# First stage of a long convolution with two MLPs: each step's load in three transfers

## Chip, cores and metric

One Trainium2 chip, one NeuronCore. The metric is the device time of one execution in microseconds (us).

## What is computed

The reference, cut to what matters:

```python
def _attn_ref(x, v, pos_emb, w1, w2):            # x, v: (2, 12480, 128); pos_emb: (12480, 64)
    h_filt = (np.maximum(pos_emb @ w1, 0.0) @ w2) * np.exp(-0.01 * pos)[:, None]
    u = x * v
    y = irfft(rfft(u, n=2 * S, axis=1) * rfft(h_filt, n=2 * S, axis=0), n=2 * S, axis=1)[:, :S]
    return x * y

h = attn_out.reshape(24960, 128) @ w_in;  out1 = np.square(np.maximum(h, 0)) @ w_out
h = out1 @ w_in2;                         out  = (h * np.cos(h)) @ w_out2
```

All arrays are float32. The sequence of 12,480 positions is transformed as 104 by 120 (`N1` by `N2`).

## The kernel before, in words

**Three stages.** The first stage makes the convolution's inputs (u = x*v and the filter h_filt, from a small MLP over the positions) and takes the transform over 104 rows. The second stage takes the transform over 120 rows, multiplies the spectra and transforms back. The third runs the last transform and the two MLPs in one long loop. Between the stages the data goes through tensors in device memory, `Bs` and `Ds`.

**The first stage** has 30 steps q (`NCH`) of two pairs each (`CB`), so 60 pairs. `load` (lines 163 to 169) brings a step's data from device memory: a tile of 128 rows, a row being 2,672 float32 = 10,688 bytes. Columns 0 to 2463 (`XVE`) hold x, v and the transform's matrix of the step and have meaning in rows 0 to 103 only; rows 104 to 127 are padding there. The last 208 columns hold the positions' features, in all 128 rows. The tiles are a ring of five slots (`LDB`): the load of step q+5 is issued right behind the second pair of step q and waits until that pair has read the slot.

The work of a step is spread over the loop (lines 260 to 285):
- `mlp1` (line 182, TensorE, then ScalarE's Relu on line 184) reads the positions. For step q it runs about three pairs behind the issue of the step's load.
- `prep` reads x and v (line 192, GpSimd's product u) and makes h_filt (line 194, TensorE; line 196, ScalarE). Its first product for step q stands four pairs ahead of that step's first pair.
- `pair` multiplies with the transform's matrix (line 210, TensorE, into three tiles `A` of PSUM), copies one half (line 212, ScalarE) and forms sum and difference (line 214, VectorE).
- `store` (line 219) writes a step's result to `Bs` as two transfers, 128 and 80 rows of 6,144 bytes. They are issued from ScalarE's own queue, between its other instructions.
- Between the pairs VectorE, ScalarE and GpSimd split the MLPs' weights; 16 transfers `wr` (line 87) of 512 KB load them.

**Order.** Each engine executes its instructions in the order of the program, and a DMA issue stands in that order too: what waits ahead of a store on ScalarE, or ahead of a load on SP, holds up all that stands behind it. Every transfer from SP and ScalarE counts on one of eight semaphores (DMAHW0 to DMAHW7), given out in turn. A transfer waits until the one that had its semaphore before has landed.

Of the kernel before, what the change touches and what calls it, by code (L numbers as in the profile page):

```python
# [21 lines left out]
N1, N2, HB = 104, 120, 60  # L22
# [3 lines left out]
NCH, CB = 30, 2  # L26
# [15 lines left out]
KE = 32  # L42
FIRST = 384 + 4 * NCH + 2 * KR
XVE, SLOT = 2048 + 2 * KR, 3072
CROSS = (1, 1)
WS = 59
INV2PI = 0.15915494309189535
# [10 lines left out]
def conv_moe(ctx, tc, t):  # L58
    nc = tc.nc
# [70 lines left out]
    def slot(name, pool=ring, size=SLOT):  # L130
        return pool.tile([128, size], F32, tag="ld", name=name)
# [16 lines left out]
    with ExitStack() as st:  # L148
# [12 lines left out]
        ld = {}  # L161

        def load(q):
            sl = slot("ld", *((ring, SLOT) if q % LDB < NB else (ring1, XVE + CB * N1)))
            nc.sync.dma_start(out=sl[:, 0:XVE + CB * N1], in_=t["ld"][q])
            x, v = (sl[0:N1, 1024 * n:1024 * (n + 1)].rearrange("p (i a d) -> p i a d", i=CB, a=2) for n in range(2))
            et = sl[0:N1, 2048:XVE].rearrange("p (a m) -> p a m", a=2)
            pt = sl[:, XVE:XVE + CB * N1].rearrange("p (i k) -> p i k", i=CB)
            ld[q] = (pt, x, v, et)
# [76 lines left out]
        def last():  # L246
            direct(NCH - 1, 1, 0)
            direct(NCH - 1, 1, 1, nc.scalar)
            store_late(NCH - 1)

        upto("load", load, LDB, NCH)
        nc.sync.dma_start(out=Bs[0:KE, CB * LATE:HB].rearrange("p x e -> p (x e)"),
                          in_=bass.AP(t["ld"].tensor, 0, [[CB * (NCH - LATE) * 768, KE], [1, CB * (NCH - LATE) * 768]]))
        nc.scalar.dma_start(out=Gt, in_=t["G"])
        nc.scalar.dma_start(out=It, in_=t["IG"])
        for n, (q, i) in enumerate(seq):
            lead = min(LA, n + 1) if n else 1
            upto("mlp", mlp1, (n + lead - 1) // CB + 1, NCH)
            upto("prep", lambda m: prep(*seq[m]), n + lead, len(seq))
            pair(q, i, last if n == len(seq) - 1 else None)  # L260
            upto("mlp", mlp1, (n + lead + 1) // CB + 1 if n else 1, NCH)
            if i == 0 and q:
                if q > LATE:
                    store_late(q - 1)
                if q < NCH - 1:
                    store(q - 1)
            if (q, i) == (LATE, 0):
                load2(0)
                load2(1)
            if (q, i) == (NCH - 1, 0):  # L270
                load_late(0, CB * (NCH - 1 - LATE))
                direct(q, 0, 0)
                direct(q, 0, 1)
            if (q, i) == (NCH - 1, 1):
                load_late(1)
                load2(2)
                store(q - 1, nc.sync)
                store(q, nc.sync)
                load_late(2)
            if i == 1:  # L280
                upto("load", load, q + LDB + 1, NCH)
            if 1 < n < WS:
                decode(2)
# [22 lines left out]
    with ExitStack() as st:  # L306
# [33 lines left out]
        def crossed(g, j, c):  # L340
            return (j, c) == CROSS and g < NG - 1

# [375 lines left out]
def tables():  # L718
    import numpy as np
    s1, k1, s2 = np.arange(N1), np.arange(N1), np.arange(N2)  # L720
    b, kk = np.arange(HB), np.arange(HB)
    n = N2 * s1[:, None, None] + s2[None, :, None]
    th = 2 * np.pi * (((4 * k1[None, None, :] - 1) * n) % (4 * S)) / (4 * S)
    E = np.stack([np.cos(th), -np.sin(th)], 2)
    T = E.transpose(3, 1, 2, 0) / S
    E = E.reshape(N1, 2, HB, 2, N1).transpose(2, 0, 1, 4, 3).reshape(HB, N1, 2 * KR)
    G = np.zeros((2 * HB, 2, 128))
    I = np.zeros((128, 2, 2 * HB))
    for c in range(2):
        p = 2 * np.pi * ((2 * b[:, None] * kk[None, :] + b[:, None] * c) % N2) / N2  # L730
        C, Z = np.cos(p), np.sin(p)
        for n, o in enumerate(turns()):
            re, im = (HB + n, n) if n % CB and n > 1 else (n, HB + n)
            G[re, c, 0:60], G[im, c, 0:60] = C[o], Z[o]
            G[re, c, 64:124], G[im, c, 64:124] = -Z[o], C[o]
        I[0:60, c, 0::2], I[64:124, c, 0::2] = C.T, -Z.T
        I[0:60, c, 1::2], I[64:124, c, 1::2] = Z.T, C.T
    f = lambda a: np.ascontiguousarray(a, dtype=np.float32)
    win = np.exp(-0.01 * np.arange(S, dtype=np.float32))
    first = np.zeros((128, FIRST))  # L740
    first[0:N1, 384 + 4 * NCH:] = E[NCH]
    win = paired(win.reshape(N1, 2, HB), 0, 2).transpose(0, 2, 3, 1)
    first[0:N1, 384:384 + 4 * NCH] = win.reshape(N1, 4 * NCH)
    return {"E": f(E[0:NCH]), "first": f(first), "G": f(G), "IG": f(I)}, T
# [6 lines left out]
def paired(a, rows, pairs):  # L751
    import numpy as np
    a = np.take(a, turns(), pairs)
    a = a.reshape(a.shape[:pairs] + (NCH, CB) + a.shape[pairs + 1:])
    m = np.moveaxis(a, (pairs, pairs + 1, rows), (0, 1, 2)).copy()
    m[1:, 1] = m[1:, 1, ::-1]
    return np.moveaxis(m, (0, 1, 2), (pairs, pairs + 1, rows))


def host(inp):  # L760
    import numpy as np
    c = np.ascontiguousarray
    out, T = tables()
    out["T"] = c(T.astype(np.float32).reshape(N1, N2 // CI, CI, 2, N1).transpose(1, 0, 2, 3, 4))
    a = inp["x"].reshape(2, N1, N2 // CI, CI, D)
    out["xT"] = c(a.transpose(2, 4, 3, 0, 1)).reshape(N2 // CI, D, CI, UT)
    for s, d in (("x", "xl"), ("v", "vl")):
        a = paired(inp[s].reshape(2, N1, 2, HB, D), 1, 3)
        out[d] = c(a.transpose(3, 1, 4, 2, 0, 5)).reshape(NCH, N1, 1024)
    xve = np.concatenate([out.pop("xl"), out.pop("vl"), out.pop("E")], 2)  # L770
    p = paired(inp["pos_emb"].reshape(N1, 2, HB, 64), 0, 2)
    pos = c(p.transpose(2, 1, 4, 3, 0)).reshape(NCH, 128, CB * N1)
    out["ld"] = np.concatenate([np.pad(xve, [(0, 0), (0, 128 - N1), (0, 0)]), pos], 2)
    for a in range(2):
        out["first"][64 * a:64 * a + 64, 64 * a:64 * a + 64] = inp["w1"]
        out["first"][64 * a:64 * a + 64, 128 + 128 * a:256 + 128 * a] = inp["w2"]
    for n in _W:
        out[n] = c(inp[n]).view(np.int64)
    return out
# [22 lines left out]
```

## Time and profile before

| | us |
|---|---|
| median of 3 runs (lowest, highest) | 2743.23 (2742.17, 2744.23) |
| profiled execution, first to last instruction (its span) | 2739.5 |
| TensorE busy in the span | 2693.9 (98%) |
| VectorE busy | 2387.9 (87%) |
| ScalarE busy | 2383.4 (87%) |
| GpSimd busy | 1351.7 (49%) |

For the profiled execution the span is all that is recorded of its time; the median of the runs is 3.7 us above it. Busy shares are means over stages with different limits: the first stage is about the first 223 us, the second ends at about 480 us, the rest is the MLPs. A profile has 16 DMA engines; a DMA share of 1 says that all 16 have work all the time.

### The profile page before, as it was taken

The numbers are of one execution on the slowest core, as the hardware profiler recorded it, in microseconds if no ns is written. First come the engines' busy times: TensorE is split into PE (matmuls) and PEld (weight loads), VectorE is DVE, ScalarE is ACT, GpSimd is POOL, SyncE is SP. The second block draws the span as 40 slices with busy tenths as digits, with TensorE's granted clock in tenths as the row PEclk, the third lists the DMA queues.
The fourth block names the chain that finished last, engine by engine and source line by source line (L and its number), as shares of the span: only waits on it lengthen the run. The fifth ranks groups of instructions, "written<-read, shape, count | busy, mean of one in ns | idle before, by whom it ended". The sixth has DMA issues, their size and how long they took to land.

```text
span 2739.5 us, 38808 instructions
## 1 busy us (share of the span) xinstructions
PE 2693.9 (98%) x11778; PEld 2112.1 (77%) x11778; DVE 2387.9 (87%) x4675; ACT 2383.4 (87%) x4295; POOL 1351.7 (49%) x1050
## 2 busy tenths in 40 slices
PE   8898999999999999999999999999999999999999
PEld 5554444888888888888888888888888888888887
DVE  5886999788888888888888888888888888888888
ACT  4445998799999999999999999999999999999998
POOL 4554888144444444444444444444444444444445
PEclk9999999999999999999999999999999999999999
DMA  9997997210101110101010101010001110101000
GB/s 380 393 396 260 297 297 243 84 31 16 35 26 32 29 33 16 35 26 32 28 32 17 38 23 32 29 32 29 31 18 32 29 32 29 32 17 32 17 8 10
DMA packets 86771, 219.64 MB, mean 80 GB/s; under 512 B 6025, under 2 KB 49633, under 8 KB 82689
## 3 DMA queue, kind: packets, MB, share of 16 engines
q1 hardware_dynamic: 79298, 180.24, 20.2%
q10 hardware_dynamic: 7263, 36.92, 3.4%
q8 instruction: 93, 1.52, 0.2%
q14 instruction: 117, 0.96, 0.1%
HBM read 140.37 MB, written 77.07 MB: 79 GB/s over the span
## 4 chain that ended last, share of the span: by engine, by line
PE 92%; DMA 5%; ACT 1%; DVE 1%; issue 1%; POOL 0%; SPq 0%; POOLq 0%; ACTq 0%; DVEq 0%
PE h L562 13%; PE h L564 13%; PE y L578 13%; PE h L563 13%; PE y L576 13%; PE y L577 13%; PE pc L528 4%; DMA ld<-ld 3%; PE d L385 3%; PE Z L345 3%; PE A L210 3%; PE H L317 2%; PE hp L194 1%; DMA B<-Bs 1%; PE hp L182 0%
## 5 line engine op out<-in xcount | busy, mean ns | idle before, releaser
L667 POOL TENSOR_TENSOR gl<-g,gh 128x512 fp32r<-128x512 f32 (+2 forms) x800 | 1040.6, 1301 | 1221.5 <-ACT gh L658 718.1
L650 DVE TENSOR_TENSOR g<-h,c 128x512 f32<-128x512 f32 (+2 forms) x800 | 537.7, 672 | 209.4 <-ACT c L642 196.9
L627 ACT ACTIVATE k<-h,quarter 128x512 int32<-128x512 f32 (+2 forms) x800 | 540.3, 675 | 122.0 <-PE h L564 118.8
L562 PE MATMUL h<-zh,wh 128*128 128x512 f32 (+2 forms) x1600 | 625.5, 391 | 1.2 <-DVE zh L546 0.9
L578 PE MATMUL y<-gl,wh 128*128 128x512 f32 (+2 forms) x1600 | 617.6, 386 | 4.3 <-POOL gl L667 2.5
L576 PE MATMUL y<-gh,wl 128*128 128x512 f32 (+2 forms) x1600 | 616.4, 385 | 0.1
L564 PE MATMUL h<-zh,wl 128*128 128x512 f32 (+2 forms) x1600 | 615.6, 385 | 0.0
L563 PE MATMUL h<-zl,wh 128*128 128x512 f32 (+2 forms) x1600 | 614.7, 384 | 0.0
L577 PE MATMUL y<-gh,wh 128*128 128x512 f32 (+2 forms) x1600 | 614.1, 384 | 0.0
L642 ACT ACTIVATE c<-r,halfpi 128x512 f32<-128x512 f32 (+2 forms) x800 | 565.3, 707 | 2.6 <-DVE r L635 2.6
L621 DVE TENSOR_TENSOR gl<-g,gh 128x512 fp32r<-128x512 f32 (+2 forms) x800 | 534.6, 668 | 1.1
L635 DVE CUSTOM_DVE_ANT_0 r<-h,k 128x512 f32<-128x512 f32 (+2 forms) x800 | 534.1, 668 | 0.0
L601 ACT ACTIVATE r<-h 128x512 f32<-128x512 f32 (+2 forms) x800 | 471.9, 590 | 69.4 <-PE h L564 57.8
L607 ACT ACTIVATE g<-r 128x512 f32<-128x512 f32 (+2 forms) x800 | 492.8, 616 | 1.0 <-DVE gl L621 0.4
L614 DVE CAST gh<-g 128x512 fp32r<-128x512 f32 (+2 forms) x800 | 330.4, 413 | 38.5 <-ACT g L607 35.6
L578 PEld LDWEIGHTS y<-gl,wh 128*128 128x128 f32 x1600 | 300.4, 188 | 70.4 <-POOL gl L667 7.7
L576 PEld LDWEIGHTS y<-gh,wl 128*128 128x128 f32 x1600 | 300.5, 188 | 60.7 <-DVE zl L589 1.2
L564 PEld LDWEIGHTS h<-zh,wl 128*128 128x128 f32 x1600 | 300.9, 188 | 59.9
L577 PEld LDWEIGHTS y<-gh,wh 128*128 128x128 f32 x1600 | 300.7, 188 | 59.4
L562 PEld LDWEIGHTS h<-zh,wh 128*128 128x128 f32 x1600 | 301.5, 188 | 56.8 <-issue 1.0
L563 PEld LDWEIGHTS h<-zl,wh 128*128 128x128 f32 x1600 | 301.2, 188 | 54.8
L658 ACT ACTIVATE gh<-g 128x512 fp32r<-128x512 f32 (+2 forms) x400 | 246.1, 615 | 0.1
(67 smaller groups left out, 2424.9 us busy)
## 6 DMA issues: line engine op xcount, KB each, us to landing
ld<-ld SPq DMA_DIRECT2D x30, 1336.0 KB
B<-Bs SPq DMA_DIRECT2D x25, 1536.0 KB
dt<-Ds SPq DMA_DIRECT2D x59, 416.0 KB
Ds<-dt SPq DMA_DIRECT2D x24, 960.0 KB
Bs<-bt ACTq DMA_DIRECT2D x28, 768.0 KB
Bs<-bt ACTq DMA_DIRECT2D x28, 480.0 KB
xt<-xT SPq DMA_DIRECT2D x60, 208.0 KB
out<-o SPq DMA_DIRECT2D x47, 256.0 KB
```

Source lines behind the costliest of these rows:

```text
L562: nc.tensor.matmul(h[:, :n], wh[:, f, :], zh[:, :n], start=True, stop=False)
L563: nc.tensor.matmul(h[:, :n], wh[:, f, :], zl[:, :n], start=False, stop=False)
L564: nc.tensor.matmul(h[:, :n], wl[:, f, :], zh[:, :n], start=False, stop=True)
L576: nc.tensor.matmul(y[:, :n], wl[:, f, :], gh[:, :n], start=a, stop=False)
L577: nc.tensor.matmul(y[:, :n], wh[:, f, :], gh[:, :n], start=False, stop=False)
L578: nc.tensor.matmul(y[:, :n], wh[:, f, :], gl[:, :n], start=False, stop=b)
L621: nc.vector.tensor_tensor(out=gl[:, :n], in0=g[:, :n], in1=gh[:, :n].bitcast(F32), op=ALU.subtract)
L627: nc.scalar.activation(k[:, :n], hp[2, u][:, :n], AF.Identity, scale=-1.0, bias=quarter)
L635: nc.vector._custom_dve(TENSOR_ADD_SAT, out=r[:, :n], in0=h[:, :n], in1=k[:, :n], s0=0.25, s1=-0.75)
L642: nc.scalar.activation(c[:, :n], r[:, :n], AF.Sin, bias=halfpi, scale=TWO_PI)
L650: nc.vector.tensor_tensor(out=g[:, :n], in0=h[:, :n], in1=c[:, :n], op=ALU.mult)
L667: nc.gpsimd.tensor_tensor(out=gl[:, :n], in0=g[:, :n], in1=gh[:, :n].bitcast(F32), op=ALU.subtract)
```

## The change

`load` issues three transfers in place of one: the positions (128 rows of 832 bytes, from a tensor `pos` of their own), then rows 0 to 95 of the other columns (`EVEN` is 96; rows of 9,856 bytes), then rows 96 to 103. The 24 rows of padding are gone from the host's tensor and from the transfer. Nothing else differs.

```diff
--- before.py
+++ after.py
@@ -42,6 +42,7 @@
 KE = 32
 FIRST = 384 + 4 * NCH + 2 * KR
 XVE, SLOT = 2048 + 2 * KR, 3072
+EVEN = N1 - N1 % 16
 CROSS = (1, 1)
 WS = 59
 INV2PI = 0.15915494309189535
@@ -162,7 +163,9 @@
 
         def load(q):
             sl = slot("ld", *((ring, SLOT) if q % LDB < NB else (ring1, XVE + CB * N1)))
-            nc.sync.dma_start(out=sl[:, 0:XVE + CB * N1], in_=t["ld"][q])
+            nc.sync.dma_start(out=sl[:, XVE:XVE + CB * N1], in_=t["pos"][q])
+            nc.sync.dma_start(out=sl[0:EVEN, 0:XVE], in_=t["ld"][q, 0:EVEN])
+            nc.sync.dma_start(out=sl[EVEN:N1, 0:XVE], in_=t["ld"][q, EVEN:N1])
             x, v = (sl[0:N1, 1024 * n:1024 * (n + 1)].rearrange("p (i a d) -> p i a d", i=CB, a=2) for n in range(2))
             et = sl[0:N1, 2048:XVE].rearrange("p (a m) -> p a m", a=2)
             pt = sl[:, XVE:XVE + CB * N1].rearrange("p (i k) -> p i k", i=CB)
@@ -770,7 +773,7 @@
     xve = np.concatenate([out.pop("xl"), out.pop("vl"), out.pop("E")], 2)
     p = paired(inp["pos_emb"].reshape(N1, 2, HB, 64), 0, 2)
     pos = c(p.transpose(2, 1, 4, 3, 0)).reshape(NCH, 128, CB * N1)
-    out["ld"] = np.concatenate([np.pad(xve, [(0, 0), (0, 128 - N1), (0, 0)]), pos], 2)
+    out["ld"], out["pos"] = xve, pos
     for a in range(2):
         out["first"][64 * a:64 * a + 64, 64 * a:64 * a + 64] = inp["w1"]
         out["first"][64 * a:64 * a + 64, 128 + 128 * a:256 + 128 * a] = inp["w2"]
```

On SP's queue the first stage looks as follows. `ld` is a step's tile, `wr` a weight tile; the brackets name the semaphores that a row waits for, and a DMAHW there is the one that the transfer then counts on itself, or that of the data it needs. Before, from the load of step 9 on:

```order
L165 DMA ld<-ld 128x2672 [waits DMAHW0_49,DMAHW7_49,PE_49,Pool_49]
L87 DMA wr<-moe_w_in 128x1024 [waits DMAHW1_49,DVE_49]
L165 DMA ld<-ld 128x2672 [waits DMAHW3_49,DMAHW4_49,PE_49,Pool_49]
L87 DMA wr<-moe_w_out 128x4x256 [waits DMAHW6_49,DMAHW2_49,DVE_49]
L165 DMA ld<-ld 128x2672 [waits DMAHW0_49,PE_49,Pool_49]
L165 DMA ld<-ld 128x2672 [waits DMAHW3_49,PE_49,Pool_49]
```

With the change, the same place:

```order
L166 DMA ld<-pos 128x208 [waits DMAHW2_49,PE_49,Pool_49]
L167 DMA ld<-ld 96x2464 [waits DMAHW3_49]
L168 DMA ld<-ld 8x2464 [waits DMAHW5_49]
L88 DMA wr<-moe_w_in 128x1024 [waits DMAHW7_49,DVE_49]
L166 DMA ld<-pos 128x208 [waits DMAHW0_49,PE_49,Pool_49]
L167 DMA ld<-ld 96x2464 [waits DMAHW2_49]
L168 DMA ld<-ld 8x2464 [waits DMAHW4_49]
L88 DMA wr<-moe_w_out 128x4x256 [waits DMAHW5_49,DVE_49]
```

Each load has become three issues. The first carries the wait for the slot (PE, Pool); each has a semaphore of its own and waits for that semaphore's last holder.

On ScalarE's queue, at a store between two pairs; `hT` is the Relu of `mlp1`, `Bs` the store, `ut` and `v` are the copies for the next pairs. Before:

```order
L184 ACTIVATE hT<-hp 128x208 [waits PE_49]
L219 DMA Bs<-bt 128x1536 [waits DMAHW5_49,DVE_49]
L219 DMA Bs<-bt 80x1536 [waits DMAHW7_49]
L196 ACTIVATE ut<-hp_466,first 104x128 [waits PE_49]
L196 ACTIVATE ut<-hp_466,first 104x128
L212 ACTIVATE v<-A 128x768 [waits PE_49,Activation_49]
L196 ACTIVATE ut<-hp_487,first 104x128 [waits PE_49,Pool_49]
```

With the change:

```order
L187 ACTIVATE hT<-hp 128x208 [waits PE_49]
L222 DMA Bs<-bt 128x1536 [waits DMAHW1_49,DVE_49]
L222 DMA Bs<-bt 80x1536 [waits DMAHW3_49]
L199 ACTIVATE ut<-hp_488,first 104x128 [waits PE_49]
L199 ACTIVATE ut<-hp_488,first 104x128
L215 ACTIVATE v<-A 128x768 [waits PE_49,Activation_49]
L199 ACTIVATE ut<-hp_511,first 104x128 [waits PE_49,Pool_49]
```

The order is the same. The semaphores are others: with five to six transfers a step in place of three to four, a semaphore's last holder is about one and a half steps back, where it was more than two. The store of 80 rows, which waits for DMAHW3 here, follows on that semaphore the load of rows 0 to 95 that stands second in SP's rows above. Over the first stage, 13 of the 28 stores of 80 rows follow a load of rows 0 to 95 in this way and 4 one of rows 96 to 103; of the 30 loads of rows 0 to 95, 15 follow a store of 80 rows. Before, no store of 80 rows followed a load; 18 of the 28 stores of 128 rows did, one that was issued more than two steps earlier.

## Rows read from the trace of the kernel before

**Rows 1.** the page: 40 slices of the span, and the chain's shares

```profile
DMA  9997997210101110101010101010001110101000
...
PE 92%; DMA 5%; ACT 1%; DVE 1%; issue 1%; POOL 0%; SPq 0%; POOLq 0%; ACTq 0%; DVEq 0%
```

**Rows 2.** busy time by stretch of the span; the columns are its first line

```profile
core 0: us, PE busy (x) PEld busy (x) DVE busy (x) ACT busy (x) POOL busy (x), PEclk, DMA share, GB/s
0.00:223.00 223.00, 196.31 (x635) 119.15 (x636) 173.25 (x220) 101.59 (x224) 115.69 (x94) 0.98 0.98 382
```

**Rows 3.** DMA queues, 40 to 205 us: packets, MB, share of 16 engines' time

```profile
q1 hardware_dynamic: 7729, 36.93, 59.0%
q10 hardware_dynamic: 5273, 28.09, 41.5%
...
ld<-ld SPq DMA_DIRECT2D x22, 1336.0 KB
```

**Rows 4.** chain that ended last, 36 to 64 us: start, length, what

```profile
40.71 2.60 PE A L210 x8
...
43.36 10.72 DMA ld<-ld
...
54.13 0.62 PE hp L182 x2
...
55.18 2.58 PE A L210 x8
...
58.20 2.58 PE A L210 x8
...
61.56 2.60 PE A L210 x8
```

**Rows 5.** PE's groups, 0 to 223 us: busy, mean ns, idle before, releasers

```profile
L182 PE MATMUL hp<-ld,first 128*128 128x208 f32 x60 | 17.9, 382 | 24.5 <-DMA ld<-ld 16.6 <-DMA first<-first 7.9
```

**Rows 6.** DMA queues, 7 to 22 us: the first loads

```profile
q1 hardware_dynamic: 648, 6.03, 97.1%
```

**Rows 7.** DMA queues, 9 to 17 us: short rows (Gt, It) on q10

```profile
q10 hardware_dynamic: 213, 0.18, 6.7%
```

**Rows 8.** DMA, 602 to 605.2 us: one transfer of 104 rows of 1,664 bytes

```profile
DMA packets 117, 0.17 MB, mean 54 GB/s; under 512 B 13, under 2 KB 117, under 8 KB 117
...
q1 hardware_dynamic: 117, 0.17, 19.1%
```

**Rows 9.** DMA, 605.3 to 610 us: a transfer of 128 rows, one of 104

```profile
DMA packets 574, 0.65 MB, mean 138 GB/s; under 512 B 29, under 2 KB 573, under 8 KB 573
...
dt<-Ds SPq DMA_DIRECT2D x1, 416.0 KB
xt<-xT SPq DMA_DIRECT2D x1, 208.0 KB
```

**Rows 10.** DMA, 717 to 718.8 us: mainly 128 rows of 1,664 bytes

```profile
q1 hardware_dynamic: 131, 0.21, 38.8%
```

**Rows 11.** the SP queue's waits, 40 to 205 us: total, times, longest

```profile
SPq L165 <- PE A L210: 122.6, 22, 10.4
```

**Rows 12.** line 165: its issues, ns min/median/max

```profile
L165 SPq DMA_DIRECT2D ld<-ld x30: 327/328/647, 0.7 to 201.0; - x30
```

**Rows 13.** waits of the engines, 40 to 205 us: total, times, longest

```profile
ACT hT L184 <- PE hp L182: 35.9, 22, 3.9
POOL ut L192 <- PE A L210: 15.7, 8, 3.3
```

## Prediction

> **What bounds the kernel now.** I read first the page: which stretch keeps the DMA engines busy, and what the chain that ended last consists of. TensorE makes up 92% of that chain and DMA 5%; the DMA engines are full in the first slices only [rows 1]. So the change, which touches the first stage alone, can move the time only by what it does there, and a later end of that stage is passed on: behind it TensorE fills the chain.
>
> Next, the first stage by itself. In its 223 us the DMA engines are busy 0.98 of the time and move 382 GB/s, while TensorE is busy 196.3 us, VectorE 173.3, GpSimd 115.7 and ScalarE 101.6 [rows 2]. From 40 to 205 us SP's queue (loads and weights) takes 59.0% of the engines' time and ScalarE's (stores) 41.5%, together all of it; 22 loads are issued there, one in 165 / 22 = 7.5 us [rows 3]. Third, the chain inside that stage: a pair ends, the load for its slot goes out, 10.72 us later it has landed, `mlp1` runs at once, and pairs follow 3.02 and 3.36 us apart until the next load [rows 4]. TensorE lost 16.6 us to such landings [rows 5]. The stage is therefore bound by the transfers' volume; TensorE alone would do a step of two pairs in 6.38 us [rows 4].
>
> **What the change removes.** Per load and engine, in steps:
> - Before: 128 rows on 16 engines are 8 rows of 10,688 bytes each. While loads ran nearly alone, 6.03 MB took 97.1% of 16 engines for 15 us, 233 us of engine time, so an engine moves 25.9 KB per us [rows 6]. A row takes 0.413 us, the 8 take 3.30 us.
> - Positions now: 8 rows of 832 bytes for each engine. The nearest row is that of the short rows of 960 and 1,024 bytes: 8 us x 16 x 6.7% = 8.6 us for 213 packets, 0.040 us each [rows 7]. That is 0.32 us per load.
> - Rows 0 to 95: 6 rows of 9,856 bytes for each engine at 0.381 us, 2.28 us.
> - Rows 96 to 103: no row of the trace shows a transfer of 8 rows. A transfer of 104 rows leaves 13 packets under 512 bytes [rows 8]; one of 128 rows and one of 104 leave 29 together, 16 and 13 [rows 9]. I read these as one completion for each engine that took part: 104 rows went to 13 engines. By that pattern 8 rows go to 8 engines, one each, 0.381 us more there. Bounds: spread evenly over all 16 they would add 0.19 us each; all on one engine, 8 x 0.381 = 3.05 us, which would make that engine slower than before by 2.35 us per load, 70 us in all. I take 8 engines, the value nearest to [rows 8, 9].
>
> So 8 engines go from 3.30 to 2.98 us per load and the others to 2.60: 0.32 and 0.70 us saved. A load or a store has landed when its last engine is done, so the 8 fuller engines set the pace: **30 loads x 0.32 = 9.6 us**.
>
> The page "DMA: Bandwidth & Descriptors" of the Trainium skill, section "Why a DMA increments its semaphore by 16 and not by 1", says that a transfer uses the largest number of engines up to 16 that divides its rows, and the lowest-numbered ones; the 13 of [rows 8] agree, and no run here shows the 8.
>
> **What it adds.** 60 issues on SP at 0.327 us [rows 12], 19.6 us in all. SP waited 122.6 us for slots between 40 and 205 us [rows 11], so they hide in a queue that is idle; if that cover went, a load's rows would start 0.65 us later. Weight issues behind them on SP move by the same amount; the chain of [rows 4] holds no weight tile. More transfers also mean more sharing of the eight semaphores: that is the first and third rival. A small benefit: `mlp1` now needs the positions alone, which come first; x and v are due about a pair later, at GpSimd's product, and that product's result only four pairs after that. GpSimd already waits for TensorE 15.7 us in that stretch [rows 13], so it has room. ScalarE's Relu, which stood 35.9 us behind `mlp1` [rows 13], would stand less. I count nothing for either, as volume sets the pace.
>
> The page "SBUF — State Buffer" of the Trainium skill, section "Summary: rules for kernel authors", speaks against the change: 128 partitions, and one DMA rather than several. Its figure of some 2 us fixed per transfer (section "The DMA setup-cost knee") would make 60 x 2 = 120 us, an estimate for transfers that wait for one another; [rows 3] shows queues that are full throughout, where such a cost would lie beside other transfers' data.
>
> **Sum.** The profiled execution's span is 2739.5 us; less 9.6 it is 2729.9. The median of the runs stands 3.7 us above the span, and I carry that over: **2733.6 us**.
>
> **The rivals.**
> 1. *The semaphores eat it (no change).* 13 of the 28 stores of 80 rows now wait on ScalarE for a load of rows 0 to 95 that was issued three pairs before, and 4 for one of rows 96 to 103. Three pairs take 1.5 x 6.38 = 9.6 us, a load 10.72 [rows 4]: ScalarE stands 1.1 us, as it stood before at the Relu. Behind the store wait the copies `ut` and `v` that TensorE's next pairs need. For it: the place is nearly the same as where the load is waited for today. Against it: TensorE has a third tile `A`, about a pair in hand, which the old wait at `mlp1` did not leave it. Then the 16.6 us [rows 5] stay: 2743.
> 2. *More than forecast.* The later due time of x and v lets the transfers fall behind TensorE by some microseconds more before anything stands, and the lighter engines run ahead. Then the wait of 16.6 us [rows 5] goes, and no more than that, since TensorE is next: 2726.6. Against it: the stores' semaphores above.
> 3. *Slower: a circle of two landings.* 15 of the 30 loads of rows 0 to 95 wait for a store of 80 rows issued three pairs before, and that kind of store waits for such a load in turn, three pairs on. Around this circle, three steps long, lie two landings whatever the engines do. At 10.72 us each [rows 4] it allows 21.4 / 3 = 7.15 us per step, under the present 7.5. It decides from 11.25 us per landing on; at 12 us a step takes 8.0 us, 0.5 more for 22 steps, 11 us: 2754. For it: three transfers share a queue with others, and each adds an issue to its wait. Against it: fewer bytes lie in the queue, and no more than eight transfers can.
> 4. *Rows 0 to 63 set the load's time (no change).* If the place in memory that rows are written to limits a load, and rows 0 to 63 share half of those places, dropping 24 upper rows frees nothing there: 8 x 0.381 + 0.32 = 3.37 us against 3.30, 2 us more in 30 loads: 2745. Against it: 104 rows of 1,664 bytes took 3.2 x 16 x 19.1% = 9.8 us, 0.09 each [rows 8], and mainly 128 such rows 1.8 x 16 x 38.8% = 11.2 us for 131 packets, 0.085 each [rows 10]; uneven coverage shows little cost.
>
> The fourth is a rule of the page "SBUF — State Buffer", section "Door 1: The DMA port swizzle": rows 0 to 63 reach 8 of 16 ports. By it the saving is nil; [rows 8, 10] speak against it for loads of that size.
>
> **How the numbers follow.** A measurement of this kernel tells about 0.2%, 5.5 us, from no change. The forecast gets 0.50, the first rival 0.15, the second 0.16, the third 0.12, the fourth 0.07. Faster by over 5.5 us: the second and nearly all of the forecast, 0.64. Same: the first, the fourth and a small rest of the forecast, 0.24. Slower: the third, 0.12. The forecast's own range goes from 2728 (half-way to what TensorE's wait allows) to 2738. The whole range takes in the second and fourth rivals, 2725 to 2745; the third and the one-engine bound stay outside.
>
> **What would show it.** Right: SP's queue moves 7.1 MB less (30 x 24 x 9,856 bytes); `mlp1`'s wait for `ld` on TensorE shrinks; the last load goes out some 8 to 10 us earlier than at 201.0 us [rows 12]; the stages behind are as long as before. The forecast's step fails if the DMA share of the stage falls well under 0.98 [rows 2] without an earlier end: then issues or semaphores set the pace. The third rival shows as ScalarE's stores and SP's loads waiting for DMA landings, with steps over 7.5 us; the fourth as rows of 9,856 bytes that take over 0.381 us each.

## Result, and the profile after

The change made the kernel slower: a median of 2784.26 us (2782.34 to 2786.24, 4 runs) against 2742.70 (2742.08 to 2744.23, 4 runs) before; ratio 1.015, 95% interval 1.0135 to 1.0165. The forecast was 2733.6, faster. The profiled span is 2784.1 us.

The whole loss lies in the first stage. First its stretches in the changed kernel: the two rows are the stage, up to the same count of matmuls as in [rows 2], which now lasts 268 us, and all that is behind it. Columns as in [rows 2].

```profile
0.00:268.00 268.00, 214.18 (x635) 129.00 (x636) 166.09 (x220) 100.54 (x224) 114.08 (x94) 0.89 0.99 291
268.00:2784.10 2516.10, 2494.82 (x11145) 1992.48 (x11143) 2215.32 (x4457) 2282.85 (x4072) 1237.47 (x956) 1.00 0.18 53
```

The same 635 matmuls take 268 us instead of 223, 45 us more; the rest takes 2516 us as before (2739.5 - 223). The DMA engines are as busy as in [rows 2], 0.99, and move 291 GB/s instead of 382. Fewer bytes, more time: that is the finding to explain. (Of the 45 us, 27 are TensorE's idle time, 53.8 us instead of 26.7, and 18 are matmuls that take longer: the 635 are busy 214.2 us instead of 196.3, at a mean granted clock of 0.89 instead of 0.98. From 40 to 50 us, behind waits, the clock stands at 0.50, the lower of its two levels. No run separates what the lower clock adds to the time.)

The DMA queues of the changed kernel, 7 to 22 us, answer to [rows 6], and those of 40 to 205 us to [rows 3]:

```profile
q1 hardware_dynamic: 764, 2.88, 97.3%
```

```profile
q1 hardware_dynamic: 8533, 26.51, 61.3%
q10 hardware_dynamic: 4549, 24.26, 38.3%
...
ld<-ld SPq DMA_DIRECT2D x18, 924.0 KB
...
ld<-pos SPq DMA_DIRECT2D x18, 104.0 KB
ld<-ld SPq DMA_DIRECT2D x18, 77.0 KB
```

In these 15 us, where little but loads runs, SP's queue moves 2.88 MB where it moved 6.03, and keeps the engines just as busy. 97.3% of 16 engines for 15 us are 233.5 us of engine time: **12.3 KB per us, where [rows 6] gave 25.9**. This number, bytes of SP's queue by its engine time from 7 to 22 us, is the measure of all that follows. From 40 to 205 us, 18 loads go out instead of 22, a step of 9.2 us instead of 7.5. In this stretch too it is the loads that are slow: SP's queue moves 16.4 KB per us of engine time where [rows 3] gives 23.7, while ScalarE's stores, of 128 and of 80 rows, keep 24.0 of 25.6.

Rows of 9,856 bytes can be read by themselves in a stretch with nothing else in it. SP's queue from 16.5 to 18 us in the changed kernel; then, from two kernels of the experiments below, from 12 to 14 us in e1 (128 rows) and from 14 to 16 us in e9 (96 rows, without the 8):

```profile
q1 hardware_dynamic: 33, 0.33, 98.4%
```

```profile
q1 hardware_dynamic: 83, 0.82, 98.6%
```

```profile
q1 hardware_dynamic: 48, 0.47, 101.0%
```

A row takes 1.5 x 16 x 98.4% / 33 = 0.72 us in the change, 0.38 in e1 and 0.67 in e9. Rows over 0.381 us are the sign that the prediction gave for its fourth rival.

What TensorE loses by it: PE's group of `mlp1` from 0 to 290 us (as [rows 5]) and the chain's shares on the page (as [rows 1]):

```profile
L185 PE MATMUL hp<-ld,first 128*128 128x208 f32 x60 | 20.8, 435 | 41.5 <-DMA ld<-pos 36.2 <-DMA first<-first 5.2
```

```profile
PE 82%; DMA 7%; ACT 7%; issue 2%; DVE 2%; POOL 0%; SPq 0%; ACTq 0%; POOLq 0%; DVEq 0%
```

TensorE's wait for landings grows from 16.6 to 36.2 us, and the transfers' share of the chain from 5% to 7% (ScalarE's 7% are mostly lines of the second stage, which is as long as before). SP's waits from 40 to 205 us (as [rows 11]) show something that could be a cause as well:

```profile
SPq L88 <- DMA Bs<-bt: 40.7, 6, 11.0
SPq L166 <- PE A L213: 18.3, 4, 10.3
SPq L166 <- DMA Bs<-bt: 16.9, 6, 5.7
SPq L167 <- DMA Bs<-bt: 14.2, 7, 7.1
```

SP waited 122.6 us for slots; now it waits for landings of stores and loads, that is for its turn at a semaphore. So two theories stand: the rows themselves go slowly (as these 15 us say), or three transfers in place of one fill the eight semaphores (rivals 1 and 3).

### The profile page after: what moved, and what is told of

Same layout as the page of the kernel before. It is cut to its first block, busy times and chain, and to the rows that moved or that the text cites. A ratio compares the mean times of both kernels' runs of the same rounds, so it can differ in the third digit from the quotient of the medians.

```text
span 2784.1 us, 38892 instructions
## 1 busy us (share of the span) xinstructions
PE 2709.0 (97%) x11778; PEld 2121.5 (76%) x11778; DVE 2381.4 (86%) x4675; ACT 2383.4 (86%) x4295; POOL 1351.5 (49%) x1050
## 4 chain that ended last, share of the span: by engine, by line
PE 82%; DMA 7%; ACT 7%; issue 2%; DVE 2%; POOL 0%; SPq 0%; ACTq 0%; POOLq 0%; DVEq 0%
PE h L565 13%; PE h L567 13%; PE y L581 12%; PE h L566 12%; PE y L579 12%; PE y L580 12%; PE pc L531 4%; DMA ld<-pos 3%; DMA Bs<-bt 3%; PE A L213 2%; ACT w L355 2%; ACT w L356 1%; ACT hr L335 1%; ACT hi L326 1%; ACT ds L393 1%
```

## Experiments

All runs in one table; each time is the median, with the ratio to the kernel before on the same chip and its 95% interval. "KB/us" is the measure above, from the rows of SP's queue from 7 to 22 us. The runs stand on several chips, on which the kernel before has medians of 2741.7 to 2743.8 us; two runs are known against each other to some 5 to 7 us. e5 to e8, e13 to e15 and e17 leave out part of the data (e5 to e8 send 1.10 MB per load, the kernel before 1.37), so they are compared with e7 and not with the kernel before.

| run | a load's transfers behind the positions | us | ratio (interval) | KB/us |
|---|---|---|---|---|
| before | (one transfer of 128 rows with the positions in it) | 2743 | 1 | 25.9 |
| change | 96 rows, 8 rows | 2784.3 | 1.015 (1.0135 to 1.0165) | 12.3 |
| e1 | 128 rows, padded | 2737.7 | 0.9982 (0.9969 to 0.9994) | 25.3 |
| e2 | 128 rows, padded, as two column halves | 2737.2 | 0.9982 (0.9970 to 0.9993) | 24.8 |
| e3 | the change's bytes as 128 rows (and 8 rows of 2,464 bytes) | 2733.7 | 0.9967 (0.9958 to 0.9977) | 23.5 |
| e4 | 104 rows | 2783.8 | 1.0140 (1.0114 to 1.0167) | 14.1 |
| e5 | 128 rows; 64 rows into partitions 0 to 63 | 2761.5 | 1.0064 (1.0039 to 1.0089) | 14.8 |
| e6 | 128 rows; 64 rows into partitions 32 to 95 | 2728.3 | 0.9944 (0.9927 to 0.9961) | 24.6 |
| e7 | 128 rows; 128 rows | 2725.8 | 0.9934 (0.9916 to 0.9952) | 24.2 |
| e8 | 128 rows; 96 rows | 2743.7 | 1.0008 (0.9998 to 1.0018) | 17.5 |
| e9 | 96 rows alone | 2754.0 | 1.0037 (1.0023 to 1.0051) | 14.8 |
| e18 | 96 rows; the 8 rows' bytes as 128 rows | 2762.4 | 1.0081 (1.0059 to 1.0103) | 14.9 |
| e16 | rows 32 to 95; rows 0 to 31 | 2757.6 | 1.0060 (1.0040 to 1.0080) | 16.6 |
| e11 | rows 32 to 95; 0 to 31; 96 to 103 | 2788.5 | 1.0170 (1.0150 to 1.0191) | 13.4 |
| e10 | 128 rows, then the positions last | 2755.4 | 1.0046 (1.0032 to 1.0061) | 25.1 |
| e12 | e1 again, beside e10 | 2736.0 | 0.9983 (0.9972 to 0.9994) | 25.3 |
| e17 | e7 and one transfer of 8 rows | 2738.2 | 0.9983 (0.9972 to 0.9993) | 21.3 |
| e13 | e7 and four of 8 rows, neighbours | 2777.7 | 1.0122 (1.0105 to 1.0139) | 19.3 |
| e14 | e7 and four of 8 rows, 12 partitions apart | 2783.1 | 1.0137 (1.0119 to 1.0155) | 20.2 |
| e15 | e7 and four of 16 rows, 4 partitions apart | 2763.1 | 1.0081 (1.0061 to 1.0102) | 20.1 |

### Rows or transfers: the changed kernel's parts put back

The first run keeps the positions apart and brings the padding back:

```diff
-            nc.sync.dma_start(out=sl[0:EVEN, 0:XVE], in_=t["ld"][q, 0:EVEN])
-            nc.sync.dma_start(out=sl[EVEN:N1, 0:XVE], in_=t["ld"][q, EVEN:N1])
+            nc.sync.dma_start(out=sl[:, 0:XVE], in_=t["ld"][q])
...
-    out["ld"], out["pos"] = xve, pos
+    out["ld"], out["pos"] = np.pad(xve, [(0, 0), (0, 128 - N1), (0, 0)]), pos
```

> Two transfers a step: the positions, and all 128 rows of the other columns, padding included (the bytes of before). Theory A, the place of the rows: an engine is slow when it shares the part of on-chip memory it writes with another engine; 128 rows are spread without that, 96 and 8 are not. Then the first loads run at about 410 GB/s again (with the change 204), and the time is 2743, give or take 5 us. Theory B, the semaphores' circle: 4.5 transfers a step instead of 5.5 take away about half of the loss: 2755 to 2770 us, the first loads still under 350 GB/s.

The second keeps three transfers, each of 128 rows:

```diff
+            nc.sync.dma_start(out=sl[:, 0:XVE // 2], in_=t["ld"][q, :, 0:XVE // 2])
+            nc.sync.dma_start(out=sl[:, XVE // 2:XVE], in_=t["ld"][q, :, XVE // 2:XVE])
...
```

> Three transfers a step as in the change, with the same turns of the semaphores, but all of 128 rows: positions, and the other columns in two halves of 4,928 bytes a row, padding included. Theory A (place of the rows): 2743 to 2752 us, DMA at 380 to 395 GB/s from 40 to 205 us. Theory B (semaphores): 2780 to 2790 us, as the change, or more, since it moves 21% more bytes.

The third sends the bytes of rows 0 to 95, from the same place of device memory, as 128 rows of 7,392 bytes, and 8 rows of 2,464 bytes behind them:

```diff
+            nc.sync.dma_start(out=sl[:, 0:1848], in_=bass.AP(t["ld"].tensor, q * N1 * XVE, [[1848, 128], [1, 1848]]))
+            nc.sync.dma_start(out=sl[EVEN:N1, 1848:XVE], in_=t["ld"][q, EVEN:N1, 1848:XVE])
...
```

> The change with the bytes of rows 0 to 95 sent as 128 rows of 7,392 bytes, from the same place in device memory, in the same number of transfers; the last transfer of 8 rows carries 2,464 bytes a row. The values stand in other rows, so the convolution's results are not the reference's; the amount of work is. Theory A (place of the rows): the saving that was forecast appears: 2730 to 2738 us. Theory B (semaphores): 2775 to 2785 us. Theory C, reading rows at a pitch of 9,856 bytes from device memory or fewer bytes per transfer is what is slow: also about 2780, as the source's addresses are the same ones.

The fourth sends the 104 rows in one transfer (`out=sl[0:N1, 0:XVE], in_=t["ld"][q]`).

> Two transfers a step: the positions, and rows 0 to 103 in one, without padding. By the short packets of the 104-row transfer before, 13 engines take 8 rows each. Theory A (place of the rows): neighbours in rows share a part of the memory again, so rows of 9,856 bytes take well over 0.38 us: 2765 to 2800 us. Theory B (semaphores): as the kernel with 128 rows in two transfers, 2750 to 2770. If neither the place nor the semaphores matter: 13 engines with 8 x 0.381 + 0.32 us, as before: 2743.

SP's queue from 7 to 22 us in the four, first the padded one, the column halves, the 128 rows of the change's bytes, then 104 rows:

```profile
q1 hardware_dynamic: 1305, 6.01, 99.0%
```

```profile
q1 hardware_dynamic: 1816, 6.03, 101.5%
```

```profile
q1 hardware_dynamic: 1493, 5.73, 101.4%
```

```profile
q1 hardware_dynamic: 580, 2.73, 80.4%
```

Whatever is sent as 128 rows goes at 23 to 25 KB per us. Three transfers with the change's turn through the semaphores lose nothing (2737.2), and SP's longest wait from 40 to 205 us is for slots again. The first row is that of the column halves, the other two are the longest of the padded one:

```profile
SPq L166 <- PE A L213: 61.4, 19, 5.6
```

```profile
SPq L166 <- DMA ld<-ld: 46.1, 12, 6.0
SPq L166 <- PE A L212: 41.7, 14, 5.2
```

Both still wait for landings too, some 50 us in all with the halves and some 70 in the padded one, at no loss. So the number of transfers and SP's waits for their turn are not what failed. Both runs are even 5 to 6 us faster than the kernel before, and faster than expected (2743, and 2743 to 2752). The change's own bytes from their own place of memory take 2733.7 when they are written as 128 rows, the forecast's figure; so it is not the source. One transfer of 104 rows, without one of 8, is as slow as the change. Its 80.4% is near 13/16 = 81%: 104 rows keep 13 engines busy, as read from [rows 8].

### Where the rows are written

To test the place alone, four kernels send the same 0.47 MB per load as a third transfer that nobody reads, behind the positions and 128 rows of 4,096 bytes. The first has 64 rows in partitions 0 to 63, the second the same in 32 to 95, the third 128 rows, the fourth 96 rows. The diff is that of the first; the second writes `sl[32:96, 1232:3072]`:

```diff
+            nc.sync.dma_start(out=sl[:, 1024:1232], in_=t["pos"][q])
+            nc.sync.dma_start(out=sl[:, 0:1024], in_=t["ld"][q, :, 0:1024])
+            nc.sync.dma_start(out=sl[0:64, 1232:3072], in_=t["ld"][q, 0:64, 0:1840])
...
```

> Each load here is the positions, 128 rows of 4,096 bytes that every reader uses (v and E are read from x's columns, so the convolution's values are not the reference's), and a third transfer that nobody reads: 64 rows of 7,360 bytes into partitions 0 to 63. Theory A (place of the rows: a transfer of 64 rows gives each of 16 engines 4 rows in a row; by the port table of the Trainium skill two engines then write each of 8 ports at the same time) expects the third transfer at half rate: five loads are 0.53 + 2.62 + 2.36 MB; 3.15 MB at 410 GB/s and 2.36 MB at 205 take 19.2 us, so from 7 to 22 us SP's queue moves about 4.3 MB instead of over 5.4 at full share. Per step the engines need 1.15 us more than with 128 rows, about 7.4 us against TensorE's 6.4 to 6.5: some 20 us over the control, near 2752. Theory B (any transfer of fewer rows than 128 is slow, wherever it is written) expects the same here and in the run with partitions 32 to 95. Theory C (64 or 96 rows by themselves cost nothing; only the transfers of 104 and of 8 rows were slow) expects this run like the control, 2732.

> As the run before, with the 64 rows of 7,360 bytes in partitions 32 to 95; nothing else differs, same bytes, same rows per engine, same source. Theory A: by the port table partitions 32 to 63 lie on the 8 even ports and 64 to 95 on the 8 odd ones, and 4 rows in a row are one port, so each engine has a port to itself: as fast as 128 rows, over 5.4 MB from 7 to 22 us, TensorE waiting for the first load only, 2732 (2730 to 2735). Theory B: as slow as with partitions 0 to 63, about 2752. Theory C: 2732.

> The control: the third transfer's bytes as 128 rows of 3,680 bytes. All theories: full rate, 5.5 MB within 7 to 22 us (about 13.5 us of work), TensorE waits for the first load only, some 2732 (2730 to 2735), as in the run that sent the change's bytes as 128 rows.

> The third transfer as 96 rows of 4,896 bytes into partitions 0 to 95 (0.47 MB as in the other three), as the change places its rows 0 to 95, without a transfer of 8 rows behind it. Theory A: two or more engines on one port for most of the time; if the 96 rows were what slowed the change (204 GB/s), they go at about half rate here as well: some 4.3 MB from 7 to 22 us and near 2750. If the 8 rows were the culprit, this run is nearer to the control. Theory B: about 2752. Theory C: 2732.

SP's queue from 7 to 22 us, in the same order:

```profile
q1 hardware_dynamic: 1264, 3.58, 100.8%
```

```profile
q1 hardware_dynamic: 1802, 5.43, 92.1%
```

```profile
q1 hardware_dynamic: 2210, 5.97, 102.9%
```

```profile
q1 hardware_dynamic: 1573, 4.28, 101.9%
```

Moved by 32 partitions, the same transfer goes from 14.8 to 24.6 KB per us and the kernel from 2761.5 to 2728.3 us, 33 us, as fast as 128 rows within the intervals. Only the place differs, so for these 64 rows the place is shown to set the rate: their rows of 7,360 bytes take 0.28 us in the median in partitions 32 to 95 and 0.59 in 0 to 63. 96 rows lie between the two (17.5 KB per us, 18 us over the control). The expectation had this right in sign and order; the sizes were off: 64 rows in partitions 0 to 63 were put near 2752 and took 2761.5, 96 rows near 2750 and took 2743.7. The control and the 64 rows in 32 to 95 were put at 2730 to 2735; both came out faster.

The Trainium skill has a map for this. The page "SBUF — State Buffer", section "Door 1: The DMA port swizzle", assigns partitions 0 to 31 and 32 to 63 to the same 8 of 16 ports and 64 to 127 to the other 8; the page "DMA: Bandwidth & Descriptors", section "The descriptor swizzle", says that in a transfer of 128 partitions each engine has one port to itself. If the engines take 64 rows in order, four each (no trace shows which engine takes which row), then by the map rows 32 to 95 give each engine a port as well, and rows 0 to 63 put two engines on each of eight. The pair e5 and e6 agrees with both. That the 96 and the 104 rows are slow for the same reason is argued from it: no run moves them to another place whole.

### The 8 rows

The change without its third transfer (rows 96 to 103 left out of the products):

```diff
-            nc.sync.dma_start(out=sl[EVEN:N1, 0:XVE], in_=t["ld"][q, EVEN:N1])
...
-        nc.tensor.matmul(A[a][:, m, 0:384], turned(q, i, a)[:, SPLIT * m:SPLIT * m + 128], u[:, i, a, :],
+        nc.tensor.matmul(A[a][:, m, 0:384], turned(q, i, a)[:, SPLIT * m:SPLIT * m + 128], u[0:EVEN, i, a, :],
```

> The changed kernel without the transfer of rows 96 to 103: the products of GpSimd and TensorE run over rows 0 to 95 only (rows 96 to 103 are left out of the convolution; TensorE streams as many columns as before). From 40 to 205 us the change took 165 / 18 = 9.2 us for a step, the kernel before 7.5. Theory A1 (both transfers lose by sharing a place: 8 rows in partitions 96 to 103 lie on two ports by the port table, four engines on each, 4 x 0.381 us on 8 of 16 engines, 0.76 us of the mean engine per load): a step falls to 8.1 to 8.4 us, 18 to 27 us less in some 25 to 30 steps: about 2760. Theory A2 (the 96 rows carry nearly all of the loss): only 8 of 104 rows' time goes, some 0.3 us per step: about 2776. Theory A3 (the 8 rows are the main loss): near 2740.

And that kernel with the third transfer's bytes as 128 rows of 616 bytes:

```diff
+            nc.sync.dma_start(out=sl[:, 2672:2826], in_=bass.AP(t["ld"].tensor, (q * N1 + EVEN) * XVE, [[154, 128], [1, 154]]))
...
```

> The changed kernel with its third transfer's bytes (those of rows 96 to 103) sent as 128 rows of 616 bytes to columns that nobody reads; products over rows 0 to 95 only (rows 96 to 103 are left out), as in the run without the third transfer (2754). Three transfers per load, the same bytes and semaphores as the change (2784). Theory A (rows set the time: 8 rows of 9,856 bytes are a seventh slow row for 8 engines and set them out of step with the others): here only some 8 x 0.03 us per engine and load come on top, 2755 to 2763. Theory D (a third transfer and its semaphore cost the 30 us): 2775 to 2790.

SP's queue, 7 to 22 us, without the third transfer, and with it as 128 rows:

```profile
q1 hardware_dynamic: 917, 3.46, 97.6%
```

```profile
q1 hardware_dynamic: 1225, 3.52, 98.2%
```

Now the loss can be laid out as a ladder: 2736.0 with positions apart and padding (e12); 2754.0 when 96 rows take the place of 128 and nothing else is sent (18 us more, for 25% fewer bytes of rows); 2762.4 with the third transfer's bytes as 128 short rows (8 us; 30 loads x 8 rows an engine x 0.024 to 0.040 us by [rows 6, 7] are 6 to 10); 2784.3 when the same bytes are 8 long rows (22 us more). By the ratios of the table the three steps are 15, 12 and 19 us, each known to some 5 to 7, so the shares are rough. The form of the 8 rows costs about 20 us beyond their bytes and their transfer, nearly half of the loss of 42; as 128 rows the bytes behave as theory A expected (2755 to 2763). Without the 8 rows, 2754.0 lies between what A1 and A3 expected (2760 and 2740).

In the 15 us from 7 to 22 this can be followed per load. 1.13 MB at 12.3 KB per us are 92 us of engine time, 5.75 for each of 16 engines; without the 8 rows 1.05 MB at 14.8 are 4.44, with them as 128 rows 1.13 MB at 14.9 are 4.74. 8 rows at 0.381 us on 8 engines would have been 0.19 in the mean; they cost 1.3. Only part of this is their own time. The positions' rows, 0.059 us in the mean without them, take 0.092 with them. Of the change's 343 rows of 9,856 bytes in the first 22 us, 36 took over 0.9 us, one in ten, where without the 8 rows and with them as 128 none did; the 8 rows are one in thirteen, and the trace does not tell which rows the 36 are.

Why, four runs tried to tell. They add to the control of 128 rows one or four small transfers per load that nobody reads, 29,440 bytes each: 8 rows in neighbouring partitions, 8 rows 12 partitions apart (by the map of the Trainium skill, on 8 different ports), 16 rows of half the length 4 partitions apart.

```diff
...
+            for n in range(4):
+                nc.sync.dma_start(out=sl[72 + 8 * n:80 + 8 * n, 2152:3072], in_=t["ld"][q, 8 * n:8 * n + 8, 0:920])
```

This is the first (e13). The second (e14) writes `sl[n:n + 85:12, 2152:3072]`, the third (e15) 16 rows to `sl[32 + n:93 + n:4, 2152:2612]`, the single transfer (e17) `sl[96:104, 2152:3072]`.

> The control of 128 rows (positions, 128 rows of 4,096 and 128 rows of 3,680 bytes; 2725.8 us) with four more transfers per load, of 8 rows of 3,680 bytes each, that nobody reads, into neighbouring partitions 72 to 79, 80 to 87, 88 to 95 and 96 to 103. By the port table of the Trainium skill each such transfer lies on two ports, four engines on each. Theory A (engines that write one place share its rate): four transfers take 4 x 4 x 0.142 = 2.3 us of 8 engines, 1.1 of the mean engine, where a place for each engine would take 0.57 and 0.28. The control's step is at TensorE's pace with the DMA engines nearly full, so most of it shows: 25 to 30 steps of 1 to 1.7 us, 2755 to 2775. Theory B (a transfer of 8 rows costs its issue, semaphore turn and its 8 engines, wherever it goes): the same as with the rows apart.

> The same four transfers of 8 rows of 3,680 bytes, with the 8 rows 12 partitions apart (0, 12, ... 84; then 1, 13, ... and so on), so that by the port table each of the 8 engines has a port to itself. Same bytes, same number of rows, engines, issues and semaphores. Theory A: 4 x 0.142 = 0.57 us on 8 engines, a step of some 7.3 us at most, 2728 to 2742. Theory B: as slow as the rows together.

> The runs with four transfers of 8 rows of 3,680 bytes (2778 and 2783, rows together or apart) with the same bytes as four transfers of 16 rows of 1,840 bytes, 4 partitions apart from 32 to 95, so that all 16 engines take part with one row each on ports of their own. If the 8 engines that alone carry 8 rows were the cause: 8 us over the control at most, 2726 to 2736. If the number of transfers was (seven per load through eight semaphores; from 7 to 22 us those runs had the engines busy 0.79 and 0.85 only): as slow as they, 2765 to 2785, with the engines' share from 7 to 22 us under 0.9 again.

> The control of 128 rows (2725.8) with one extra transfer of 8 rows of 3,680 bytes to partitions 96 to 103 instead of four: four transfers per load. If each small transfer costs the same: a quarter of 52 us, 2739. If it is the turn through eight semaphores that is filled by seven transfers per load and not by four: 2726 to 2731.

Rows apart brought no gain: 2777.7 together, 2783.1 apart, where the theory of the place expected 2728 to 2742; 16 rows, by the map on all engines and each on a port of its own, still took 2763.1, between the two expectations (up to 2736, from 2765). So the place of the 8 rows is not shown to be what they cost. It is not refuted either, as these runs have another limit than the change. SP's queue from 7 to 22 us with four transfers of 8 rows together, and SP's waits from 40 to 205 us:

```profile
q1 hardware_dynamic: 1694, 3.86, 83.2%
```

```profile
SPq L167 <- DMA Bs<-bt: 22.9, 8, 4.7
SPq L170 <- DMA Bs<-bt: 15.6, 16, 1.8
SPq L166 <- DMA ld<-ld: 14.0, 13, 1.8
```

The engines are not full (83% and less, where the change had 97%), and SP stands before line after line for a landing, its turn at a semaphore. Rows that lie apart also take SP longer to issue, 1.3 us more per load with four transfers, so the pair differs in more than the place. Line 170, 8 rows together, then apart (min, median, max ns):

```profile
L170 SPq DMA_DIRECT2D ld<-ld x120: 272/293/1301, 2.1 to 248.3; - x120
```

```profile
L170 SPq DMA_DIRECT2D ld<-ld x120: 622/623/1529, 2.1 to 255.0; - x120
```

A single transfer of 8 rows costs 12 us over the control (2738.2 against 2725.8, expected 2739 if each cost the same), where its engines' time at 25.9 KB per us is 30 x 0.142 = 4.3. The 12 are known to some 6. It is a quarter of the 52 us that four cost, as if each cost the same, so the loss of the four is not shown to come from the turn of the semaphores. So a small transfer costs nearly three times its bytes even with four transfers per load and engines that are full.

The packets from 7 to 22 us tell where this time is not. In e15 the small rows of 1,840 bytes took 0.078 us in the mean, 24 KB per us; slow are the transfers behind them, rows of 4,096 bytes with 0.226 us in the mean where the control has 0.171. In e17 these took 0.206. What in a small transfer does so (half the engines taking part, the place, or engines that get out of step) stays open.

### Dividing the rows by place

If the place alone set the rate, the change's rows could be divided so that 64 of them run unhindered: rows 32 to 95 first, then 0 to 31, with rows 96 to 103 and without (there rows 96 to 103 are left out of the products).

```diff
+            for a, b in ((32, 96), (0, 32), (96, N1)):
+                nc.sync.dma_start(out=sl[a:b, 0:XVE], in_=t["ld"][q, a:b])
```

> The changed kernel with the same 104 rows divided otherwise: positions, then rows 32 to 95 (64 rows), 0 to 31 and 96 to 103, each to its own partitions; no padding, the same bytes, one transfer more. Theory A: rows 32 to 95 at full rate (4 x 0.381 = 1.5 us per engine), rows 0 to 31 with two engines on each of 8 ports (2 rows x 2 x 0.381 = 1.5), 8 rows 0.76 in the mean, positions 0.3: 4.1 us per load, where the change took about 4.7 (5.6 us of its step for SP's queue, of which weights about 0.95). A step of some 8.5 us instead of 9.2: 2762 to 2772, faster than the change and slower than the kernel before. If the place does not matter and only that a transfer has fewer than 128 rows, or the number of transfers does: 2784 or more.

> The run without rows 96 to 103 (2754) with its 96 rows divided: rows 32 to 95 in one transfer, rows 0 to 31 in another; the same bytes, three transfers per load as in the change. Theory A by place: 4 rows at 0.381 and 2 rows at twice that, 3.05 us per load and engine where the 96 rows in one took 6 x 0.65 = 3.9: 2738 to 2748. If dividing a load by rows sets the engines out of step, as the same division with 8 rows more (2788) may show: 2754 or more.

Both missed. With the 8 rows 2788.5, no better than the change; without them 2757.6, no better than 96 rows in one transfer (2754.0). SP's queue of the latter from 7 to 22 us:

```profile
q1 hardware_dynamic: 1072, 4.09, 102.8%
```

16.6 KB per us instead of 14.8: the first loads take 11% less engine time, not the 22% expected (3.05 us for 3.9), and the whole kernel gains nothing. Rows 32 to 95 are two thirds of the rows, yet of the 461 rows of 9,856 bytes in the first 22 us only 177 took under 0.4 us. The likely reading, not shown, is that a clean transfer does not stay clean when others that share places run beside it; how much of the rest is the further transfer, no run separates.

### Why the padded version is faster than the kernel before

The version of positions and 128 padded rows moves the bytes of the kernel before and is 0.2% faster. Its reverse sends the rows first:

```diff
-            nc.sync.dma_start(out=sl[:, XVE:XVE + CB * N1], in_=t["pos"][q])
             nc.sync.dma_start(out=sl[:, 0:XVE], in_=t["ld"][q])
+            nc.sync.dma_start(out=sl[:, XVE:XVE + CB * N1], in_=t["pos"][q])
```

> The version of positions and 128 padded rows, with the order of its two transfers reversed: the rows first, the positions behind them. It tells why that version was 0.2% faster than the kernel before. If it is because mlp1 needs the positions alone and these land first: here mlp1 waits for the last bytes of the load again, TensorE stands at mlp1 some 24 us as in the kernel before, and the time is 2743 (2740 to 2746), no change against the kernel before. If the gain came from something else about two transfers (more semaphores, a finer division of the queue): 2738, as with the positions first.

> The version of positions and then 128 padded rows once more, in more rounds, on the same chip as the reversed order: 2738, 0.2% faster than the kernel before, if the earlier result holds; and by about 5 us faster than the reversed order if the positions' early landing is the reason.

PE's group of `mlp1`, 0 to 290 us, positions last, then first:

```profile
L184 PE MATMUL hp<-ld,first 128*128 128x208 f32 x60 | 18.2, 387 | 32.5 <-DMA ld<-pos 32.5
```

```profile
L184 PE MATMUL hp<-ld,first 128*128 128x208 f32 x60 | 16.6, 358 | 10.4 <-DMA ld<-pos 6.1 <-DMA first<-first 4.3
```

Same transfers, other order: 2755.4 against 2736.0, and TensorE's wait at `mlp1` is 32.5 us against 10.4. So the order, and with it the early landing, is worth 19 us between these two. That it also makes the padded version faster than the kernel before fits (TensorE waits 24.5 us at `mlp1` there [rows 5]), but no run shows it by itself: positions last were expected at 2743, as before, and are 12 us slower than that. A second transfer that lands behind the rows is worse than one transfer with all of it. This version (e1, e12), faster than before by 0.17% (0.06 to 0.28 by e12) and than the change by 1.7%, and e2, which equals it, are the fastest of the versions that leave nothing out.

## Why the prediction was wrong

**What bounds the kernel** held in part. The stage is bound by transfers, a later end of it is passed on whole (45 us in the stage, 44.6 in the span), and the stages behind are as long as before. But it is bound by the transfers' time and not, as the prediction has it, by their volume. Of its signs the smaller volume came (382 GB/s for 223 us are 85 MB, 291 for 268 are 78); `mlp1`'s wait grew, and the last load went out at 247.4 us instead of 201.0.

**The step that failed** is "6 rows of 9,856 bytes for each engine at 0.381 us". The 25.9 KB per us of [rows 6] were taken for a property of an engine; they hold for loads of 128 rows, and nearly (24.6) for a mix with 64 rows in partitions 32 to 95. For the change's transfers the engines give 12.3 in the same window, and a row of 9,856 bytes takes 0.72 us. 96 rows alone give 14.8; 96 rows of 4,896 bytes pull a mix with 128-row transfers down to 17.5. At 25.9 KB per us the change's load should have taken 1.13 MB / 25.9 / 16 = 2.7 us of the mean engine, and takes 5.75. The padding is not idle cargo: with it the engines keep their rate. Why is shown for 64 rows (the place they are written to) and argued for the 96.

**The 8 rows** were bounded at 0.19 to 3.05 us and taken at 0.381 us on 8 engines. They cost 1.3 us of the mean engine in the first loads, and leaving them out gives back 30 us, 1 us for each of 30 loads. That 8 engines take part held: when the loads are done, SP's queue has moved 1,472 packets of 4 bytes, the completions of [rows 8], in the change and 1,232 in e9, 240 more or 8 for each load. So it was the time of a row, and what the 8 rows do to the others, that was far too low; the bound held, but it was left outside the range because one engine with all 8 rows seemed the only way to get there.

**The saving by volume** was right where rows are spread: e3 moves the change's bytes and takes 2733.7, the forecast's own number. But 5 to 6 of its 9 us come with the early positions (e1, e12), for which the prediction says "I count nothing"; the padding's bytes bring only 2 to 4 us more (against e12 and e1), a difference known to some 4. So the 9.6 us are one term that was missed and one that was too high, and the sum fits by luck.

**The rivals.** The second, TensorE's wait gone and 2726.6, is where e7 stands (2725.8), which leaves out still more bytes; the change never came near. The first and third, semaphores: SP waits for landings as the third said (ScalarE hardly: 1.9 us of its waits from 40 to 205 us are for landings), and the DMA share did not fall. But e2 has the same turn and loses nothing, and e18's third transfer costs little more than its bytes. The third's sign came, its mechanism is not what cost the time. The fourth named the place: "rows 0 to 63 share half of those places". It got 0.07 and a price of 2 us, as it counted only how many rows each place gets in total, which is the same for 96 rows as for 128: 3.37 us per load and engine by its sum, where 4.44 were measured in the mean engine even without the 8 rows. Its evidence against, [rows 8, 10], was no test: there single transfers of short rows ran with engines 19% and 39% busy, and 128 rows (0.085 us each) and 104 (0.09) were both at 18 to 20 KB per us, below the 25.9 of [rows 6], which tells of short rows and not of the place.

**The rule of the Trainium skill** that the prediction set aside (page "SBUF — State Buffer", section "Summary: rules for kernel authors": 128 partitions, and one transfer rather than several) was right in its first half, by 47 us here (the change against e1). Its second half did not show: three transfers of 128 rows were as fast as two and faster than one.

**The range**, 2725 to 2745, left out every case in which rows of another number than 128 go at another rate. No row of the trace showed such a load beside full engines, and the bound for that, from below and above, was not drawn. The stores of 80 rows in [rows 3] do not fill the gap: with those of 128 rows they go at 25.6 KB per us, so it is not the number of rows alone that makes a transfer slow.

## What to carry to other kernels

Before padding is cut from a load that shares full DMA engines, ask at which rate the remaining rows go: here 96 rows in place of 128 took the engines from 25.9 to 14.8 KB per us, and 8 rows sent on their own to 12.3. Take an engine's rate from a transfer of the same shape and direction, or keep the shape (128 rows) and cut the rows' length. What a stage waits for first (here 106 KB of 1.37 MB) gains by its own transfer ahead of the rest, and loses by one behind it.

## Not expected of the hardware

- A transfer of 64 rows of 7,360 bytes: 14.8 KB per us of engine time in its window when it is written to partitions 0 to 63, 24.6 when to 32 to 95.
- The engines read as busy 0.97 to 1.01 at half to six tenths of their rate (change, e5, e9): the DMA share does not tell full speed from standing in each other's way. GB/s beside the share does (291 at 0.99, 382 at 0.98).
- 8 rows per load, 7% of its bytes, sent alone cost 30 us, where the whole change lost 42.
- Stores of 128 and 80 rows kept 24.0 KB per us beside the change's slow loads, where they had 25.6.
- An issue on SP takes 293 ns for 8 neighbouring partitions and 623 ns for 8 that lie 12 apart.
